# A gated linear recurrence with a ReGLU layer behind it, on one core: one store a chunk, six output buffers, a new instruction order

## The chip, the core and the metric

The kernel runs on one core of a Trainium2 chip. The core has a matrix engine (TensorE, PE in the profile; its weight loads are PEld), a vector engine (VectorE, DVE), a scalar engine (ScalarE, ACT), a general engine (GpSimd, POOL) and a queue engine (SyncE, SP), which here only issues DMA transfers. Each engine works through its own list of instructions in order and waits on semaphores for the others. The metric is the device time of one execution in microseconds (us).

## What is computed

A recurrence over 768 time steps for 4 batches and 8 heads of width 48, and a ReGLU layer of width 1536 over its 3072 output rows of width 384:

```python
f = 1.0 / (1.0 + np.exp(-f_logit))
for t in range(S):
    state = f[:, :, t, :, None] * state + np.einsum('bhd,bhe->bhde', k[:, :, t], v[:, :, t])
    y[:, :, t] = np.einsum('bhd,bhde->bhe', q[:, :, t], state)
x = y.transpose(0, 2, 1, 3).reshape(B * S, H * D)
out = (np.maximum(x @ w_gate, 0.0) * (x @ w_val)) @ w_out
```

Inputs, weights and output are float32 in memory; the matrix products run in bfloat16.

## The kernel before

**Recurrence.** The rows are cut into chunks of 128 time steps, 24 chunks in all; two chunks of one batch make a unit, and the twelve units run in the order of their time, batch by batch (`seq`). `unit(u)` loads f, k, q and v of a unit (4 buffers each), takes exp and logarithm of the gate on ScalarE, sums the logarithms along time with triangular matmuls (L537 to L539, "cumsum"), takes exponentials of the sums (L555, L562), multiplies them onto k and q ("hats", L574 and L580), transposes the result (units 0 to 3 on TensorE, L612, the others by DMA on SP, L623), forms scores (L637), masks them (`ptm`, L646 to L651) and adds the product of scores and v to the product of q and the state (`out_of`, L735 to L746). A decay total per chunk (L674, L678 and the exponential at L683, or a small round trip by DMA) updates the state (L498 to L505).

**Even and odd rows.** A partition of a loaded tile holds two neighbouring time steps. For the chunks in `PE_X` the copy of the result (`xT`) puts the rows back in the order of time; for the other eight the result is transposed by DMA (L765) with the 64 even rows ahead of the 64 odd ones, and the output keeps that order until it is stored.

**ReGLU.** Four chunks make a group; `ffn_hidden(g, r0, r1, j)` makes one of twelve slices of 128 hidden columns: three gate matmuls into a PSUM bank, three value matmuls into another (both L783), relu on ScalarE (L788) and the product on VectorE into `gT` (L790). `ffn_out` makes a chunk's output from twelve slices (L807, four steps of three matmuls), copies the bank to an output buffer `osb` (L393 on ScalarE, L394 on VectorE) and stores the buffer on SP's queue (L828). Chunk `w` uses buffer `w % NO`, with `NO = 4`; the last chunk is done in two pieces of 256 and 128 columns. A chunk in `PE_X` is stored by one transfer of 128 rows, each other chunk by two transfers of 64 rows with a stride of two rows.

**Order.** Nothing is ordered by the code's sequence: each step is entered in a list with what it reads and writes (`Plan.add`), and the constants give the rest. `SEQUENCE` has the order of the steps on each engine, by their numbers; `HOMES` the order in which tiles use the eight PSUM banks; `UNITS` the engine for each copy or product (a name ending in 1 is a copy done as a reduction on VectorE); `FILLERS` the number of matmuls of zeros (L861) that run before a step's other waits; `FIRST` the first loads, with `x@y` for a weight slice x that is issued only once load y has landed. `follow` checks that the lists agree, and `needs` derives the semaphore waits. Weights are loaded by GpSimd's queue (L467), as it converts them to bfloat16; all other transfers are on SP's queue (loads: L453).

At the start VectorE writes the constants (L381, L409, L421), among them `zeros`, which the fillers and one further matmul of zeros into a bank of its own (`hot`, L854) read; that matmul stands in TensorE's list behind the first transposes of unit 0.

Of the kernel before, what the change touches and what calls it, by code (L numbers as in the profile page):

```python
# [37 lines left out]
class Plan:  # L38
# [82 lines left out]
    def needs(self, warm):  # L121
# [69 lines left out]
    "ACT": [  # L191
# [9 lines left out]
    "DVE": [  # L201
# [9 lines left out]
    "POOL": [  # L211
# [38 lines left out]
FILLERS = {67: 4, 105: 1, 82: 4, 89: 4, 86: 1, 124: 1, 127: 1, 151: 1}  # L250
# [23 lines left out]
def bass_hgrn2_outer__then__ffn_reglu_kernel(  # L274
# [11 lines left out]
    C = 128  # L286
# [3 lines left out]
    DM, DFF = w_gate.shape  # L290
# [142 lines left out]
    for i in range(NV):  # L433
        fill(fill_on["vpad"][i], f"vpad{i}", bass.AP(tensor=vpad[i], offset=D, ap=[[VW, 128], [VSTEP, NP], [1, 16]]).bitcast(U32), 0, 32)
# [508 lines left out]
```

## Time and profile before

| | |
|---|---|
| time, median of 3 runs | 193.91 us (192.78 to 194.66) |
| time of the profiled execution | 193.92 us |
| its span, first to last instruction | 192.2 us |
| VectorE, ScalarE, GpSimd busy | 126.2, 116.0, 98.9 us |
| DMA | 32.40 MB, mean 169 GB/s |
| stores of the output | 33 transfers: 15 of 192 KB, 16 of 96 KB, one of 128 KB and one of 64 KB |

The span is cut into 40 equal slices in the page's second part; a digit is the busy share of an engine in that slice, in tenths. TensorE's matmuls are pipelined and their ends are modelled, so its busy time overstates its work. In a timeline each row has the start, the duration, the engine, the line, the operation, the written and read tiles, the shape and the number of merged instructions, and in brackets the idle time of the engine before it and what ended it. "SPq" and "POOLq" are the queues that issue transfers.

### The profile page before, as it was taken

The numbers are of one execution on the slowest core, as the hardware profiler recorded it, in microseconds if no ns is written. First come the engines' busy times: TensorE is split into PE (matmuls) and PEld (weight loads), VectorE is DVE, ScalarE is ACT, GpSimd is POOL, SyncE is SP. The second block draws the span as 40 slices with busy tenths as digits, with TensorE's granted clock in tenths as the row PEclk, the third lists the DMA queues.
The fourth block names the chain that finished last, engine by engine and source line by source line (L and its number), as shares of the span: only waits on it lengthen the run. The fifth ranks groups of instructions, "written<-read, shape, count | busy, mean of one in ns | idle before, by whom it ended". The sixth has DMA issues, their size and how long they took to land.

```text
span 192.2 us, 4338 instructions
## 1 busy us (share of the span) xinstructions
PE 179.4 (93%) x1708; PEld 97.8 (51%) x1708; DVE 126.2 (66%) x233; ACT 116.0 (60%) x227; POOL 98.9 (51%) x132
## 2 busy tenths in 40 slices
PE   0988899999999999989999989999999999999982
PEld 0455674456545464545554535555555554554552
DVE  2589877886797899877784979585177424235501
ACT  4976787894858978975887763682343332224020
POOL 5496756897689679858688994115403200000000
PEclk9999999999999999999999999999999999999999
DMA  6999999999999999999998979532602103000145
GB/s 158 325 290 241 216 230 211 268 172 163 275 285 202 210 327 275 193 213 257 258 293 194 226 151 171 127 82 41 151 3 63 42 0 102 3 0 0 45 119 164
DMA packets 81199, 32.40 MB, mean 169 GB/s; under 512 B 73366, under 2 KB 81180, under 8 KB 81180
## 3 DMA queue, kind: packets, MB, share of 16 engines
q1 hardware_dynamic: 76380, 28.60, 62.3%
q0 software_dynamic: 4800, 3.54, 12.3%
q8 instruction: 13, 0.21, 0.5%
q14 instruction: 6, 0.05, 0.1%
HBM read 25.96 MB, written 4.73 MB: 160 GB/s over the span
## 4 chain that ended last, share of the span: by engine, by line
PE 58%; DMA 21%; SPq 8%; POOL 5%; ACT 2%; issue 2%; DVE 2%; POOLq 0%; ACTq 0%; DVEq 0%
PE ps L783 35%; PE ps L807 16%; DMA out_dram<-osb 7%; DMA k_in<-in_k_dram 6%; DMA wv<-in_moe_w_val_dram 5%; SPq L453 5%; DMA q_in<-in_q_dram 3%; SPq L828 2%; PE ps L637 2%; POOL hats L580 2%; PE ps L735 1%; POOL ptm L648 1%; SPq L623 1%; PE ps L746 1%; ACT relu L788 1%
## 5 line engine op out<-in xcount | busy, mean ns | idle before, releaser
L790 DVE TENSOR_TENSOR gT<-relu,ps 128x512 bf16<-128x512 bf16 (+1 forms) x75 | 47.7, 661 | 21.6 <-PE ps L783 17.4
L788 ACT ACTIVATE relu<-ps 128x512 bf16<-128x512 f32 (+1 forms) x75 | 41.4, 578 | 28.9 <-PE ps L783 17.3
L783 PE MATMUL ps<-xT,wv 128*128 128x512 bf16 (+1 forms) x225 | 55.7, 371 | 0.2 <-DMA wv<-in_moe_w_val_dram 0.2
L783 PE MATMUL ps<-xT,wg 128*128 128x512 bf16 (+1 forms) x225 | 54.8, 371 | 1.1 <-DVE hats L574 0.5
L807 PE MATMUL ps<-wo,gT 128*128 128x384 bf16 (+2 forms) x300 | 52.4, 320 | 0.7 <-ACT osb L393 0.7
L807 PEld LDWEIGHTS ps<-wo,gT 128*128 128x128 bf16 x300 | 28.1, 98 | 20.5 <-ACT osb L393 1.1
L783 PEld LDWEIGHTS ps<-xT,wg 128*128 128x128 bf16 x225 | 21.0, 98 | 23.0 <-DVE hats L574 0.7
L783 PEld LDWEIGHTS ps<-xT,wv 128*128 128x128 bf16 x225 | 20.8, 98 | 21.0 <-issue 0.7
L648 POOL TENSOR_TENSOR ptm<-ptm,seen 128x512 bf16<-128x512 bf16 x21 | 23.9, 1156 | 14.6 <-ACT ptm L646 14.3
L505 POOL TENSOR_TENSOR st<-ssum,dec 128x384 bf16<-128x384 f32 x16 | 13.2, 829 | 18.8 <-DVE ssum L502 11.3
L580 POOL TENSOR_TENSOR hats<-q_in,expo 64x384 bf16<-64x384 f32 x20 | 19.9, 996 | 4.1 <-ACT expo L555 2.2
L651 DVE TENSOR_TENSOR ptm<-ps,seen 128x512 bf16<-128x512 f32 x27 | 17.5, 685 | 2.8 <-PE ps L637 2.5
L394 DVE COPY osb<-ps 128x384 f32<-128x384 f32 (+2 forms) x11 | 5.7, 521 | 20.4 <-PE ps L807 13.5
L580 DVE TENSOR_TENSOR hats<-k_in,ps 64x384 bf16<-64x384 f32 x32 | 17.6, 551 | 1.9 <-ACT ps L562 0.8
L393 ACT ACTIVATE osb<-ps 128x384 f32<-128x384 f32 x14 | 6.7, 490 | 18.7 <-DMA out_dram<-osb 9.9
L646 ACT ACTIVATE ptm<-ps 128x512 bf16<-128x512 f32 x21 | 12.0, 597 | 5.1 <-PE ps L637 5.1
L394 POOL CAST vpad<-v_in 64x384 bf16<-64x384 f32 x20 | 10.5, 524 | 4.3 <-DMA v_in<-in_v_dram 3.3
L555 ACT ACTIVATE expo<-ps 128x384 f32<-128x384 f32 x22 | 10.2, 496 | 1.7 <-DVE ps L544 1.6
L861 PE MATMUL ps<-zeros 128*128 128x512 bf16 x17 | 6.1, 455 | 5.4 <-DVE halves L421 4.6
L574 POOL TENSOR_TENSOR hats<-q_in,expo 128x384 bf16<-128x384 f32 x9 | 9.2, 1032 | 3.3 <-ACT expo L555 2.3
L523 ACT ACTIVATE f_in<-f_in 128x768 f32<-128x768 f32 x12 | 10.0, 839 | 1.5 <-DMA f_in<-in_f_logit_dram 1.4
L562 ACT ACTIVATE ps<-ps 128x384 f32<-128x384 f32 x22 | 10.6, 499 | 0.0
(89 smaller groups left out, 182.0 us busy)
## 6 DMA issues: line engine op xcount, KB each, us to landing
f_in<-in_f_logit_dram SPq DMA_DIRECT2D x12, 384.0 KB, 6.0
v_in<-in_v_dram SPq DMA_DIRECT2D x12, 384.0 KB, 5.0
k_in<-in_k_dram SPq DMA_DIRECT2D x12, 384.0 KB, 4.8
q_in<-in_q_dram SPq DMA_DIRECT2D x12, 384.0 KB, 4.9
out_dram<-osb SPq DMA_DIRECT2D x15, 192.0 KB, 3.1
out_dram<-osb SPq DMA_DIRECT2D x16, 96.0 KB, 2.2
wg<-in_moe_w_gate_dram POOLq DMA_DIRECT2D x4, 288.0 KB, 6.8
wv<-in_moe_w_val_dram POOLq DMA_DIRECT2D x4, 288.0 KB, 7.6
```

The costliest lines, as they stand in the source:

```text
L394: return engine[e].tensor_copy(out, src)
L505: add(e, lambda: engine[e].tensor_tensor(t4(s_new), t4(tmp), rate, ALU.mult), [key] + dk, [f"S{b}_{y}"], **(dict(occ=0.79, lat=0.1) if e = ...
L555: add("ACT", lambda: sc.activation(expo[:, ei, i, 0, :], bc[i].ap[:, 0:HD], AF.Exp, scale=-1.0), [bc[i]], [f"expq{ei}_{i}"], **act_t(HD))
L562: add("ACT", lambda i=i, ex=ex: sc.activation(bc[i].ap[:, 0:HD] if in_place else ex[:, 1, :], bc[i].ap[:, 0:HD], AF.Exp, scale=1.0), [bc[i ...
L580: op = add(e, lambda i=i, n=n, x=x, e=e, y=y, lo=lo, exps=exps: engine[e].tensor_tensor(hats[64 * i:64 * i + 64, hi, y, x, :, 0:D], by_i[n ...
L646: add("ACT", lambda pt=pt, s=sj[j]: sc.activation(pt, s.ap[:, :].rearrange("p (n t) -> p n t", n=NP), AF.Copy), [sj[j]], [f"raw{mis[y]}_{j ...
L648: add("POOL", lambda pt=pt, mask=mask: gp.tensor_tensor(pt, pt, mask, ALU.mult), [f"raw{mis[y]}_{j}", "seen"], [f"raw{mis[y]}_{j}", f"ptm{ ...
L651: add("DVE", lambda pt=pt, mask=mask, s=sj[j]: ve.tensor_tensor(pt, s.ap[:, :].rearrange("p (n t) -> p n t", n=NP), mask, ALU.mult), [sj[j ...
L783: mm = te.matmul(bank.ap[:, 0:n], wt[:, kt, j * 128:(j + 1) * 128], xT[xi][:, kt, n0:n1], start=(kt == 0), stop=(kt == NK - 1))
L788: add("ACT", lambda: sc.activation(relu[ri][:, 0:n], gate.ap[:, 0:n], AF.Relu), [gate], [f"relu{ri}"], **act_t(n))
L790: add("DVE", lambda: ve.tensor_tensor(gT[gi][:, j, n0:n1], relu[ri][:, 0:n], val.ap[:, 0:n], ALU.mult), [val, f"relu{ri}"], [f"gT{gi}_{j}_ ...
L807: mm = te.matmul(bank.ap[:, 0:cut[1] - cut[0]], gT[gi][:, j, r * C:(r + 1) * C], wo[:, j, cut[0]:cut[1]], start=(j == 0), stop=(j == NJ - 1))
```

## The change

- Each chunk's output is stored by one transfer. For a chunk with even rows ahead of odd ones, the target has three dimensions (two row parities, 64 rows, columns).
- `NO` is 6: chunk `w` uses buffer `w % 6`.
- The matmul of zeros into a bank of its own is entered before the units, is the first step in TensorE's list, and the cumsums of unit 0 come after it.
- `SEQUENCE`, `HOMES`, `UNITS`, `FILLERS` and the weight releases in `FIRST` are replaced throughout. There are eight steps fewer on SP. On SP the first loads run f0 v0 f1 v1 q0 k0 k1 f2 q1 in place of f0 f1 v0 k0 q0 k1 q1 f2 v1. The decay totals of units 0 and 1 stand third and seventh in TensorE's list, ahead of the first transposes. On VectorE `zeros` is the eighth step, where it was the seventh.

```diff
-FILLERS = {67: 4, 105: 1, 82: 4, 89: 4, 86: 1, 124: 1, 127: 1, 151: 1}
+FILLERS = {67: 4, 106: 1, 83: 11, 123: 2, 87: 1, 152: 1}
...
-FIRST = 'f0 k0 q0 v0 f1 k1 q1 v1 f2 k2 q2 v2 f3 k3 q3 v3 wg0 wv0 wg1@q0 wv1@k2 wg2 wv2@k1 wg3@k0 wv3@k2 wo0@q3 wo1@v1 wo2@f1 wo3@f3'
+FIRST = 'f0 k0 q0 v0 f1 k1 q1 v1 f2 k2 q2 v2 f3 k3 q3 v3 wg0@k0 wv0@k0 wg1@q1 wv1 wg2@k1 wv2@k2 wg3@q1 wv3 wo0@f2 wo1@k0 wo2@q2 wo3@k1'
...
-    NO = 4
+    NO = 6
...
+    WARM = 512
+    hot = Bank("hot")
+    first_pe = add("PE", lambda: te.matmul(hot.ap[:, 0:WARM], zeros[:, 0:128], zeros[:, 0:WARM]), ["zeros"], [hot], occ=0.2, opens=[hot])
...
-            add("PE", cum, bkeys + ["upto", "below"], [bc[i]], occ=0.17 if on["sum"] else 0.33, lat=PE_L,
+            add("PE", cum, bkeys + ["upto", "below"], [bc[i]], after=[first_pe] if u == 0 else [], occ=0.17 if on["sum"] else 0.33, lat=PE_L,
...
-                for i in range(1 if w in pe_x else 2):
-                    whole = w in pe_x
-                    dst = bass.AP(tensor=out.tensor, offset=base + i * DM, ap=[[DM if whole else 2 * DM, C if whole else C // 2], [1, wide]])
-                    src = osb[oi][:, cut[0]:cut[1]] if whole else osb[oi][64 * i:64 * i + 64, cut[0]:cut[1]]
-                    op = add("SP", lambda dst=dst, src=src: sy.dma_start(dst, src), [f"osb{oi}_{n}"], [f"out{w}_{i}_{n}"],
-                             occ=0.36, lat=0.9)
-                    dma(op, f"osb{oi}_{i}_{n}", (0.6 if whole else 0.42) * wide / DM, 1)
+                if w in pe_x:
+                    dst = bass.AP(tensor=out.tensor, offset=base, ap=[[DM, C], [1, wide]])
+                    src = osb[oi][:, cut[0]:cut[1]]
+                else:
+                    dst = bass.AP(tensor=out.tensor, offset=base, ap=[[DM, 2], [2 * DM, C // 2], [1, wide]])
+                    src = osb[oi][:, cut[0]:cut[1]]
+                op = add("SP", lambda dst=dst, src=src: sy.dma_start(dst, src), [f"osb{oi}_{n}"], [f"out{w}_{n}"], occ=0.36, lat=0.9)
+                dma(op, f"osb{oi}_{n}", 0.6 * wide / DM, 1)
...
-    WARM = 512
-    hot = Bank("hot")
-    add("PE", lambda: te.matmul(hot.ap[:, 0:WARM], zeros[:, 0:128], zeros[:, 0:WARM]), ["zeros"], [hot], occ=0.2, opens=[hot])
```

The replaced lists are too long to show. What the prediction uses of them it names by steps. At the end of SP's list the stores now run by chunk: 16, 17, 18, 19, 20, 22, 21 and the two pieces of 23; before, they ran 17 (second half), 18 (second), 17, 16 (second), 16, 19, 18, 19 (second), 22, 20, 21 (second), 21, 20 (second) and the two pieces of 23.

More of the change, by code (lines that the diff above doesn't have):

```diff
@@ L234 @@
-    [
-        0, 9, 11, 19, 62, 31, 37, 44, 50, 78, 82, 58, 129, 90, 119, 130, 106, 163, 144, 169, 138, 179, 172, 212, 159, 160, 188, 215, 222, 217,
-        209, 266, 232, 237, 269, 242, 273, 275, 282, 285, 287, 301, 297],
-    [
-        1, 8, 6, 5, 28, 22, 25, 34, 66, 43, 47, 51, 71, 113, 92, 93, 99, 116, 105, 143, 166, 175, 152, 150, 257, 214, 200, 207, 208, 210, 231,
-        230, 244, 265, 248, 298, 293],
-    [
-        13, 16, 18, 70, 27, 33, 67, 83, 48, 84, 56, 57, 102, 115, 110, 122, 173, 146, 178, 153, 156, 185, 226, 193, 223, 198, 262, 202, 203, 239,
-        270, 247, 274, 276, 284],
@@ L243 @@
-    [
-        308, 15, 17, 24, 38, 76, 77, 81, 85, 59, 123, 91, 97, 128, 108, 121, 174, 164, 149, 171, 147, 158, 192, 189, 196, 197, 228, 267, 236,
-        253, 240, 280, 251, 283, 278, 286, 300],
-    [
-        3, 12, 61, 30, 26, 32, 68, 41, 54, 72, 74, 112, 89, 96, 131, 104, 162, 135, 140, 167, 148, 176, 221, 154, 258, 213, 191, 218, 201, 194,
-        259, 199, 245, 238, 246, 290, 292, 294, 296, 303],
+        1, 8, 71, 13, 25, 28, 70, 38, 44, 78, 72, 52, 86, 124, 96, 132, 126, 163, 112, 142, 170, 139, 172, 159, 184, 185, 192, 227, 218, 229,
@@ new lines @@
+        228, 263, 246, 238, 245, 252, 270, 278, 289],
+    [
+        10, 61, 29, 66, 34, 43, 40, 55, 80, 56, 60, 95, 90, 94, 105, 117, 104, 123, 135, 166, 150, 147, 152, 161, 155, 259, 194, 197, 199, 268,
+        230, 232, 241, 299, 277, 303],
+    [
+        22, 3, 16, 21, 63, 30, 39, 45, 41, 48, 83, 58, 89, 91, 99, 131, 106, 169, 134, 137, 167, 181, 153, 222, 186, 190, 196, 223, 200, 203,
+        211, 239, 271, 256, 283, 301, 287, 307],
+    [
+        14, 6, 19, 62, 32, 36, 42, 53, 75, 119, 125, 100, 102, 118, 129, 164, 140, 165, 180, 176, 154, 182, 160, 183, 191, 193, 224, 205, 264,
+        208, 262, 209, 204, 240, 242, 266, 273, 285, 284, 292],
@@ new lines @@
+    [
+        11, 5, 27, 35, 37, 76, 49, 50, 73, 85, 57, 98, 116, 128, 122, 174, 141, 149, 178, 212, 157, 189, 188, 217, 202, 195, 260, 236, 243, 254,
+        248, 257, 279, 286, 280, 295, 298, 305],
+    [
+        15, 4, 20, 23, 26, 33, 65, 68, 47, 79, 81, 87, 113, 93, 120, 101, 107, 111, 175, 145, 138, 146, 173, 158, 151, 214, 201, 225, 210, 267,
+        233, 251, 272, 265, 250, 274, 294, 302, 288, 297],
+    [
+        0, 9, 12, 31, 67, 77, 46, 54, 88, 114, 97, 121, 115, 127, 133, 108, 110, 136, 143, 168, 177, 213, 162, 187, 216, 226, 207, 234, 247, 269,
+        255, 275, 290, 291, 293, 300, 296, 306],
@@ L249 @@
+    [
+        2, 7, 17, 18, 24, 64, 69, 84, 51, 82, 74, 59, 92, 130, 103, 109, 144, 171, 179, 148, 156, 221, 258, 215, 198, 219, 206, 220, 261, 235,
+        231, 237, 244, 253, 249, 281, 282, 276, 304, 308],
 ]
[L250 removed]
+FILLERS = {67: 4, 106: 1, 83: 11, 123: 2, 87: 1, 152: 1}
 UNITS = {
[3 rows of a table removed]
[L256 to L264 removed]
@@ new lines @@
+    0: {'kps': False, 'qps': False, 'q0': 'DVE', 'q1': 'POOL', 'even': 'PE', 'm00': 'DVE', 'm01': 'DVE', 'm10': 'DVE', 'tk': 'ACT', 'm11': 'DVE', 'r1': 'POOL', 'tq': 'DVE', 'v11': 'DVE1', 'v10': 'POOL', 'r0': 'DVE1', 'v01': 'DVE1', 'v00': 'DVE1', 'vb': 'DVE1', 'pr': False, 'o1': 'ACT', 'vc0': 'DVE', 'x0': 'ACT', 'x1': 'ACT', 'yy': True, 'o0': 'DVE', 'vc1': 'ACT', 'td': False, 'k0': 'DVE', 'k1': 'POOL'},
+    1: {'kps': True, 'r0': 'DVE1', 'm01': 'DVE', 'm00': 'DVE', 'tq': 'ACT', 'v11': 'DVE1', 'even': 'PE', 'tk': 'DVE', 'q1': 'POOL', 'v00': 'DVE1', 'm11': 'POOL', 'r1': 'ACT', 'm10': 'DVE', 'v01': 'POOL', 'v10': 'ACT', 'q0': 'POOL', 'qps': False, 'yy': False, 'td': False, 'vb': 'DVE', 'vc0': 'DVE', 'o0': 'ACT', 'vc1': 'DVE', 'x0': 'DVE', 'o1': 'ACT', 'x1': 'ACT'},
@@ new lines @@
+    2: {'tk': 'DVE', 'v01': 'ACT', 'kps': True, 'r1': 'ACT', 'r0': 'POOL', 'even': 'PE', 'q0': 'DVE', 'v00': 'POOL', 'v10': 'POOL', 'm00': 'DVE', 'v11': 'POOL', 'm01': 'POOL', 'm11': 'POOL', 'tq': 'DVE', 'q1': 'POOL', 'm10': 'POOL', 'qps': True, 'x0': 'ACT', 'vc1': 'ACT', 'pr': False, 'vc0': 'DVE', 'o0': 'ACT', 'x1': 'DVE', 'vb': 'POOL', 'o1': 'ACT'},
+    3: {'kps': True, 'm00': 'DVE', 'm11': 'POOL', 'v11': 'ACT', 'm10': 'POOL', 'tk': 'DVE', 'v01': 'DVE1', 'r1': 'ACT', 'tq': 'ACT', 'q1': 'POOL', 'v00': 'ACT', 'v10': 'POOL', 'q0': 'DVE', 'r0': 'POOL', 'm01': 'DVE', 'even': 'DVE', 'qps': False, 'vb': 'DVE1', 'x1': 'DVE', 'o1': 'DVE', 'vc1': 'ACT', 'pr': False, 'vc0': 'DVE', 'o0': 'ACT', 'x0': 'ACT', 'sum': 'POOL'},
@@ new lines @@
+    4: {'v10': 'POOL', 'v01': 'POOL', 'm00': 'DVE', 'q11': 'POOL', 'q00': 'POOL', 'q01': 'POOL', 'q0': 'POOL', 'kps': True, 'even': 'DVE', 'm01': 'DVE', 'v00': 'POOL', 'm10': 'POOL', 'q10': 'POOL', 'q1': 'POOL', 'm11': 'POOL', 'v11': 'ACT', 'qps': False, 'tq': 'DVE', 'r0': 'ACT', 'tk': 'DVE', 'r1': 'ACT', 'yy': True, 'o1': 'ACT', 'o0': 'ACT', 'x1': 'ACT', 'x0': 'DVE', 'sum': 'POOL'},
+    5: {'q1': 'POOL', 'm00': 'DVE', 'kps': True, 'q11': 'POOL', 'v10': 'ACT', 'v00': 'ACT', 'even': 'DVE', 'q01': 'POOL', 'm11': 'POOL', 'q00': 'POOL', 'q0': 'POOL', 'v11': 'POOL', 'm01': 'DVE', 'q10': 'POOL', 'v01': 'ACT', 'm10': 'DVE', 'tq': 'ACT', 'r0': 'ACT', 'tk': 'DVE', 'r1': 'POOL', 'qps': False, 'o1': 'DVE', 'x0': 'DVE', 'o0': 'ACT', 'yy': False, 'x1': 'ACT', 'sum': 'DVE'},
@@ new lines @@
+    6: {'v10': 'POOL', 'v01': 'POOL', 'q10': 'POOL', 'm10': 'DVE', 'kps': True, 'q1': 'POOL', 'even': 'DVE', 'q01': 'POOL', 'm00': 'POOL', 'm01': 'POOL', 'q11': 'POOL', 'q00': 'POOL', 'm11': 'POOL', 'qps': False, 'q0': 'POOL', 'pr': False, 'o0': 'DVE', 'yy': False, 'o1': 'DVE', 'v11': 'POOL', 'x0': 'DVE', 'v00': 'ACT', 'x1': 'DVE', 'sum': 'POOL'},
+    7: {'v10': 'DVE1', 'kps': True, 'q1': 'POOL', 'v01': 'DVE1', 'q11': 'POOL', 'm00': 'DVE', 'v11': 'ACT', 'even': 'DVE', 'm10': 'POOL', 'm11': 'DVE', 'm01': 'POOL', 'q10': 'POOL', 'qps': False, 'q01': 'POOL', 'q0': 'POOL', 'o0': 'ACT', 'x1': 'ACT', 'td': True, 'x0': 'ACT', 'o1': 'ACT', 'v00': 'DVE1', 'sum': 'POOL'},
@@ new lines @@
+    8: {'m10': 'DVE', 'v11': 'ACT', 'q01': 'POOL', 'm01': 'POOL', 'even': 'DVE', 'q0': 'POOL', 'v10': 'ACT', 'q1': 'POOL', 'm00': 'DVE', 'kps': True, 'q11': 'POOL', 'q00': 'POOL', 'qps': False, 'v00': 'POOL', 'q10': 'POOL', 'v01': 'POOL', 'pr': False, 'td': True, 'x0': 'DVE', 'o1': 'ACT', 'x1': 'ACT', 'o0': 'ACT', 'sum': 'POOL'},
+    9: {'v11': 'POOL', 'v10': 'ACT', 'even': 'DVE', 'kps': True, 'q1': 'POOL', 'm10': 'DVE', 'v00': 'ACT', 'm11': 'POOL', 'q11': 'POOL', 'm00': 'DVE', 'q00': 'POOL', 'q10': 'POOL', 'q0': 'POOL', 'q01': 'POOL', 'v01': 'ACT', 'm01': 'DVE', 'yy': False, 'x0': 'ACT', 'td': True, 'o0': 'DVE', 'x1': 'DVE', 'o1': 'DVE', 'sum': 'POOL'},
@@ new lines @@
+    10: {'m00': 'POOL', 'm10': 'POOL', 'q0': 'POOL', 'kps': True, 'q10': 'POOL', 'm01': 'POOL', 'q11': 'POOL', 'q00': 'POOL', 'v11': 'ACT', 'even': 'DVE', 'v01': 'ACT', 'v00': 'DVE1', 'q01': 'POOL', 'q1': 'POOL', 'm11': 'DVE', 'v10': 'DVE1', 'td': True, 'o0': 'DVE', 'x0': 'DVE', 'x1': 'DVE', 'o1': 'ACT', 'sum': 'POOL'},
+    11: {'q0': 'POOL', 'v01': 'DVE1', 'q10': 'POOL', 'm00': 'DVE', 'q01': 'POOL', 'm11': 'POOL', 'q1': 'POOL', 'q00': 'POOL', 'kps': True, 'v11': 'DVE1', 'm01': 'DVE', 'q11': 'POOL', 'even': 'DVE', 'v00': 'ACT', 'm10': 'POOL', 'v10': 'ACT', 'yy': True, 'o1': 'ACT', 'td': True, 'x0': 'DVE', 'x1': 'DVE', 'o0': 'ACT', 'sum': 'POOL'},
```

15 lines of the change are left out of this document (removed), and 85 rows, old and new, of tables (SEQUENCE, UNITS).

## The prediction

> **What bounds the kernel now.** I read the page first, then the waits of TensorE, then the timeline of its end, its middle and its start.
>
> ```profile
> span 192.2 us, 4338 instructions
> ...
> PE 179.4 (93%) x1708; PEld 97.8 (51%) x1708; DVE 126.2 (66%) x233; ACT 116.0 (60%) x227; POOL 98.9 (51%) x132
> ...
> PE   0988899999999999989999989999999999999982
> ...
> PEclk9999999999999999999999999999999999999999
> ```
>
> TensorE is the engine that is full: only the first slice (4.8 us each) and the last are empty, and no other engine passes two thirds. The matrix products stay the same in the change, so what can be won or lost is time in which TensorE does not work: the start, the pauses, and the end behind its last matmul. The waits of TensorE name the pauses (waiting line, releaser: us in total, times, longest):
>
> ```profile
> PE ps L861 <- DVE halves L421: 4.6, 1, 4.6
> PE ps L807 <- ACT osb L393: 0.7, 1, 0.7
> ...
> PE ps L783 <- DVE osb L394: 0.5, 1, 0.5
> ```
>
> Two of them end with a copy into an output buffer (osb), and so are about the part that gets six buffers. The end, as a timeline (start, duration, engine, line; in brackets the idle time before and what ended it), and the row of the store line in that stretch (min/median/max ns, first and last start):
>
> ```profile
> 180.01 10.44 SPq L828 DMA_DIRECT2D out_dram<-osb  x15
> ...
> 180.84 5.04 PE L807 MATMUL ps<-wo,gT 128*128 128x384 bf16 x30
> ...
> 186.04 0.87 ACT L393 ACTIVATE osb<-ps 128x384 f32<-128x384 f32 x2 [0.81 <-DMA out_dram<-osb]
> ...
> 186.58 2.15 PE L807 MATMUL ps<-wo,gT 128*128 128x256 bf16 x24 [0.70 <-ACT osb L393]
> 188.11 0.43 DVE L394 COPY osb<-ps 128x256 f32<-128x256 f32 x1 [6.37 <-PE ps L807]
> 188.78 0.29 DVE L394 COPY osb<-ps 128x128 f32<-128x128 f32 x1 [0.24 <-PE ps L807]
> ```
> ```profile
> L828 SPq DMA_DIRECT2D out_dram<-osb x15: 338/597/604, 180.0 to 190.0; - x15
> ```
>
> Fifteen stores queue on SP from 180.01, each holding the queue 0.597 us. ScalarE's copy at 186.04 needs a buffer whose store is in that queue; TensorE needs the PSUM bank that this copy empties and pauses 0.70 us. The last copy is over at 188.78 + 0.29 = 189.07, but the last store starts at 190.0, since others are ahead of it.
>
> **The change part by part.** The sum is made against the profiled execution's own time, 193.92 us: its span of 192.2 and 1.72 around it; the median of the runs shown, 193.91, is the same.
>
> *End: one store a chunk, six buffers, new order.* The last eight chunks (16 to 23) made fifteen stores; now they make nine. Chunk 20 to 23 take buffers 2 to 5, last used by chunks 14 to 17, whose stores stand well ahead. So the copy at 186.04 has nothing to wait for: -0.70. At the very end the queue holds chunks 20, 22 and 21 and the two pieces of 23, one store each; at 0.6 us each they are through when the last copy ends: 190.0 - 189.07 = 0.93, less an issue gap: -0.9. Both pieces of 23 now go to ScalarE in place of VectorE; whole-chunk copies take 0.87 us for two there, so I put that at 0. Together -1.6; it could be 0 only if another queue took SP's place, and I see none.
>
> *One store in place of two, elsewhere.*
>
> ```profile
> out_dram<-osb SPq DMA_DIRECT2D x15, 192.0 KB, 3.1
> out_dram<-osb SPq DMA_DIRECT2D x16, 96.0 KB, 2.2
> ```
>
> Eight chunks lose one issue each, 8 x 0.597 = 4.8 us of SP's time. SP is seldom the last to be waited for, so that is not on the path. A buffer is free 3.1 us after one issue, where it was free 0.6 + 2.2 = 2.8 after the first of two: 0.3 later, under the cover of two more buffers; without them it would be paid at each osb wait.
>
> *Middle.*
>
> ```profile
> 80.71 1.30 SPq L623 DMA_TRANSPOSE qkT<-hats  x1
> ...
> 82.15 0.62 PE L637 MATMUL ps<-qkT 48*128 48x128 bf16 x16 [0.45 <-issue]
> 82.66 0.56 DVE L394 COPY osb<-ps 128x384 f32<-128x384 f32 x1 [1.10 <-DMA out_dram<-osb]
> ...
> 83.28 0.82 PE L783 MATMUL ps<-xT,wg 128*128 128x512 bf16 x3 [0.50 <-DVE osb L394]
> ```
> ```profile
> 108.96 0.49 ACT L393 ACTIVATE osb<-ps 128x384 f32<-128x384 f32 x1 [1.25 <-DMA out_dram<-osb]
> ...
> 111.18 0.40 PE L637 MATMUL ps<-qkT 48*128 48x128 bf16 x8 [0.38 <-DVE ssum L502]
> ...
> 111.88 0.40 PE L637 MATMUL ps<-qkT 48*128 48x128 bf16 x8 [0.30 <-ACT relu L788]
> ```
>
> VectorE's copy at 82.66 waited 1.10 for a store, and TensorE 0.50 behind it for the bank. With six buffers the chunk needs a store two chunks older: -0.50. At 82.15 TensorE waits 0.45 for scores whose transpose went out late on SP, and at 111 it waits 0.38 + 0.30 for engines held up by ScalarE's 1.25 for a store. These 1.13 us hang on the store queue only in part: between 0 and -1.13 I take half, -0.57.
>
> *Start.* What moves: the zeros' matmul opens TensorE's list, v0 and v1 go ahead of q0 and k0 on SP's queue (k0 from the fourth load to the sixth), weights are released by other loads, and both decay totals of units 0 and 1 go ahead of the first transposes.
>
> ```profile
> 3.09 1.15 SPq L453 DMA_DIRECT2D k_in<-in_k_dram  x1
> ...
> 4.57 1.89 PE L861 MATMUL ps<-zeros 128*128 128x512 bf16 x4 [4.57 <-DVE halves L421]
> ...
> 5.21 0.84 ACT L530 ACTIVATE bneg<-f_in 128x768 bf16<-128x768 f32 x1
> ...
> 5.48 1.15 SPq L453 DMA_DIRECT2D k_in<-in_k_dram  x1
> ...
> 8.35 1.00 POOL L574 TENSOR_TENSOR hats<-k_in,expo 128x384 bf16<-128x384 f32 x1 [0.70 <-ACT expo L562]
> ...
> 9.15 1.03 PE L861 MATMUL ps<-zeros 128*128 128x512 bf16 x4
> 9.31 1.31 POOL L574 TENSOR_TENSOR hats<-q_in,expo 128x384 bf16<-128x384 f32 x1
> ...
> 10.57 0.93 POOL L467 DMA_DIRECT2D wg<-in_moe_w_gate_dram  x1
> ...
> 11.19 0.61 PE L612 MATMUL ps<-ident,hats 128*128 128x128 bf16 x8 [0.34 <-DVE hats L574]
> ...
> 11.49 0.78 POOL L467 DMA_DIRECT2D wv<-in_moe_w_val_dram  x1
> ...
> 12.32 0.50 POOL L394 CAST vrest<-v_in 64x384 bf16<-64x384 f32 x1
> 12.91 1.96 POOL L574 TENSOR_TENSOR hats<-q_in,expo 128x384 bf16<-128x384 f32 x2
> ```
> ```profile
> 16.64 0.17 PE L674 MATMUL ps<-away,other 128*128 128x16 bf16 x1
> 16.67 0.34 PE L678 MATMUL ps<-halves,bneg 128*128 128x4 bf16 x8
> ```
>
> Zeros earlier are worth 0: the first product with data needs the logarithm, which ends at 5.21 + 0.84 = 6.05 and is not touched. The first four zero products took 1.89 us at 4.57 and 1.03 at 9.15: TensorE runs at half pace for its first 4.5 us. [...]
>
> The decay total of unit 0 stood beside a wait already; that of unit 1 at 16.64 lay in TensorE's busy stretch: -0.3 (0 to -0.7).
>
> Against this stands k0. Its load is issued in the place of 5.48 in place of 3.09, 2.39 us later. Landing times of k in the first 40 us, and of the value weights:
>
> ```profile
> DMA to landing us min/median/max: 4.8/7.1/10.9
> ```
> ```profile
> DMA to landing us min/median/max: 6.9/7.6/10.1
> ```
>
> With the shortest landing, k0 was there at 7.9, ahead of the product at 8.35, and will be at 10.3. On POOL the k product (1.00) and the q product (1.31) follow: 12.6, where TensorE began the q transposes at 11.19: +1.4. Eleven filler products, not four, stand ahead of the k transposes for it; behind them the lists hold four fillers where eight stood, and four cost 1.03 us by the row at 9.15. Part of those filled a wait, so I count 0.75 of it as won. So +0.65, between 0 (TensorE would wait for the first weights anyway) and +2.4 (the whole delay). Queued behind k0's wait are, on POOL, vrest and the weights, on VectorE the k products of unit 1; the release of wg0 by k0 adds nothing, since the k product stands ahead of it on POOL.
>
> *Everything else that was reordered* does the same work with the same matmuls. Its cost is only new or lost pauses; I take 0, with -1 to +2 about it.
>
> Sum: -1.6 - 0.50 - 0.57 - 0.3 + 0.65 = -2.3, so 193.92 - 2.3 = **191.6 us**.
>
> **The rivals.**
>
> *The store queue gets a new wait (no change).* Chunk 5's store now stands only three places ahead of chunk 11's on SP, and both use buffer 5. So chunk 11's copy, on VectorE, waits out 3.1 us of chunk 5's landing, and behind chunk 11's store stand the transposes of unit 11. For it: every osb wait above is of this kind. Against: unit 11 has other chunks' output between it and its need. Paid by half, +1.6: 193.2 (192.6 to 194.7).
>
> *The first value weights come late (slower).* With k0 at 10.3, POOL issues wg0 at 10.3 + 1.00 + 1.31 + 0.50 = 13.1 and, behind 0.93 of that issue and the two q products of unit 1 (1.96), wv0 at 16.0 in place of 11.49. It lands at 23.6 by the median, 26.1 by the longest.
>
> ```profile
> 20.45 0.49 PE L783 MATMUL ps<-xT,wv 128*128 128x256 bf16 x3
> ```
>
> That is its first use now. The new list puts two more gate triples and two chunk outputs ahead of it, some 0.5 us each by this row: needed at about 20.45 + 1.4 + 2 = 23.8. At the medians it is just in time. It decides where k0 lands later than about 10.5: with k0 at its median landing (5.48 + 7.1 = 12.6) all is 2.3 later, and with wv0's longest landing another 2.5: +4.6 or so, 193.92 - 2.3 + 4.6 = 196.2 (194.0 to 198). For it: the landings scatter this much. Against: wg1, wg2 and wv1 go out sooner than before, so the stretch after it has more to work on.
>
> [...]
>
> *More goes than I count (faster still).* All of 1.13 in the middle, 0.7 of the totals, no loss at the start, and a pause or two more: 193.92 - 1.6 - 0.5 - 1.1 - 0.7 = 190.0 (188.9 to 190.6).
>
> **How the numbers follow.** Forecast (190.6 to 192.6) 0.47, new store wait 0.17, late value weights 0.18, clock 0.04, more than counted 0.14. Measurements of this kernel scatter by about 1% (192.78 to 194.66), so no change means 191.97 to 195.85. Faster: 0.34 of the forecast's 0.47 and all of the 0.14: 0.48. Slower: two thirds of the late weights and 0.02 of the store wait: 0.14. The rest, 0.38, is no change. For 8 in 10 I leave out the lower 0.06 of the best case and 0.12 of the slow one: 189.3 to 195.6.
>
> **What would show it.** TensorE without a wait on an osb copy, and no osb copy waiting for a store, show the buffers; the last store starting within 0.1 us of the last copy's end shows the end. TensorE's first q transposes at 12 to 13, and the first value product without a wait at 23 to 24, show the start; a wait on wv there longer than 1 us, or on k or q products, shows the slow rival. SP sitting at chunk 11's store, with VectorE's copy waiting for out_dram, shows the other. A new pause of TensorE over 1 us past 40 us, in a stretch I put at 0, would make the forecast wrong by a step that it did not name.

## The result and the profile after

The changed kernel takes **204.99 us** (median of 4 runs, 204.12 to 205.48) against 193.9 us of the kernel before in the same comparison: a ratio of 1.057 with a 95% interval of [1.051, 1.064]. It is slower by 11 us; the prediction had said 191.6 us, in a range that ended at 195.6. The profiled execution took 205.48 us, 11.6 more than that of before. Here and below a ratio compares the fast runs of two kernels alone while a median is over all runs, so a ratio can differ from the quotient of two medians (for the kernel with two halves the medians of 193.01 and 193.31 us would give 0.998, where the ratio is 0.991).

The page of the changed kernel, first lines, TensorE's slices, its granted clock, and the row of the stores:

```profile
span 203.8 us, 4318 instructions
...
PE 179.5 (88%) x1689; PEld 98.9 (49%) x1711; DVE 127.7 (63%) x235; ACT 118.4 (58%) x230; POOL 96.7 (47%) x127
...
PE   2887899999999999999999993999999999999600
...
PEclk9999999999999999999999997699999999999975
...
out_dram<-osb SPq DMA_DIRECT2D x23, 192.0 KB
```

TensorE's busy time is that of before (179.4). The time came in two places that the slices show (a digit is now 5.1 us): a hole at the 25th slice, near 125 us, with a granted clock of 0.7 and 0.6 there and behind it, and two empty slices at the end. Most of what follows is about these two.

The end, as a timeline, and what the DMA engines moved from 183 us to the end of the span in 40 slices of 0.52 us (GB/s):

```profile
183.81 12.11 SPq L834 DMA_DIRECT2D out_dram<-osb  x7
...
190.73 0.49 ACT L393 ACTIVATE osb<-ps 128x384 f32<-128x384 f32 x1 [3.25 <-PE ps L811]
191.38 0.38 ACT L393 ACTIVATE osb<-ps 128x256 f32<-128x256 f32 x1 [0.16 <-PE ps L811]
192.05 0.28 ACT L393 ACTIVATE osb<-ps 128x128 f32<-128x128 f32 x1 [0.29 <-PE ps L811]
```
```profile
GB/s 0 0 0 12 18 41 24 32 32 50 50 50 50 50 50 50 56 86 284 95 62 50 50 50 56 257 144 62 57 56 38 50 50 50 50 50 50 45 8 0
```

These copies into the buffers wait for TensorE's banks alone (the brackets), as forecast, and the last one ends at 192.05 + 0.28 = 192.33. But the span ends 11.5 us later, where before it ended 3.1 us after the last copy (189.07 to 192.2). In between the DMA engines do one thing: they move 50 GB/s, slice after slice. The two peaks fit the stores of plain rows in between, chunk 22 and the pieces of chunk 23. The four chunks in even-odd order that stand in this queue (18 to 21) have 4 x 196,608 bytes; at 50 GB/s that takes 15.7 us, from 184 us on. The last store starts at about 195.5, some 3 us behind the last copy, where the prediction had asked for 0.1.

The middle, as a timeline, and two windows (start and end, length, then busy time and count for PE, PEld, DVE, ACT and POOL, granted clock, DMA share, GB/s):

```profile
123.68 0.33 PE L746 MATMUL ps<-st,qkT 128*128 128x96 bf16 x4 [1.69 <-POOL st L509]
...
125.40 0.56 DVE L394 CAST xn<-ps 128x384 bf16<-128x384 f32 x1 [4.52 <-DMA xT<-xn]
...
126.01 0.50 PE L746 MATMUL ps<-st,qkT 128*128 128x96 bf16 x4 [1.80 <-DVE xn L394]
```
```profile
120.00:125.00 5.00, 2.52 (x36) 1.56 (x34) 0.69 (x1) 0.98 (x2) 0.83 (x1) 0.95 0.72 75
125.00:130.00 5.00, 3.77 (x21) 2.13 (x23) 2.73 (x5) 2.34 (x6) 0.00 (x0) 0.50 0.79 209
```

TensorE waits 1.69 us for a state and 1.80 us for a result that waits 4.52 us for a transpose; then it runs at half clock for some five microseconds. The prediction had counted no cost in this stretch.

### The profile page after: what moved, and what is told of

It is laid out like the page before. It is cut to its first block, busy times and chain, and to the rows that moved or that the text cites. A ratio compares the mean times of both kernels' runs of the same rounds, so it can differ in the third digit from the quotient of the medians.

```text
span 203.8 us, 4318 instructions
## 1 busy us (share of the span) xinstructions
PE 179.5 (88%) x1689; PEld 98.9 (49%) x1711; DVE 127.7 (63%) x235; ACT 118.4 (58%) x230; POOL 96.7 (47%) x127
## 3 DMA queue, kind: packets, MB, share of 16 engines
q0 software_dynamic: 4800, 3.54, 11.6%
## 5 line engine op out<-in xcount | busy, mean ns | idle before, releaser
L794 DVE TENSOR_TENSOR gT<-relu,ps 128x512 bf16<-128x512 bf16 (+1 forms) x75 | 48.5, 663 | 29.1 <-PE ps L787 18.4
L792 ACT ACTIVATE relu<-ps 128x512 bf16<-128x512 f32 (+1 forms) x75 | 42.2, 580 | 36.3 <-PE ps L787 25.5
L811 PE MATMUL ps<-wo,gT 128*128 128x384 bf16 (+2 forms) x300 | 54.9, 327 | 0.0
L787 PE MATMUL ps<-xT,wv 128*128 128x512 bf16 (+1 forms) x217 | 53.4, 371 | 1.0 <-DMA wv<-in_moe_w_val_dram 0.4
L811 PEld LDWEIGHTS ps<-wo,gT 128*128 128x128 bf16 x300 | 28.8, 100 | 21.5 <-issue 2.2
L652 POOL TENSOR_TENSOR ptm<-ptm,seen 128x512 bf16<-128x512 bf16 x21 | 24.0, 1154 | 14.8 <-ACT ptm L650 14.7
L393 ACT ACTIVATE osb<-ps 128x384 f32<-128x384 f32 (+2 forms) x17 | 7.9, 471 | 15.6 <-PE ps L811 13.8
L393 ACT ACTIVATE vpad<-v_in 64x384 bf16<-64x384 f32 x19 | 9.8, 517 | 1.8 <-DMA v_in<-in_v_dram 1.0
L578 POOL TENSOR_TENSOR hats<-q_in,expo 128x384 bf16<-128x384 f32 x10 | 10.2, 1027 | 0.8 <-DMA q_in<-in_q_dram 0.5
L531 POOL TENSOR_TENSOR bneg<-f_in 128x384 bf16<-128x384 f32 x8 | 8.0, 998 | 3.9 <-ACT f_in L529 3.9
L506 DVE TENSOR_TENSOR ssum<-ps,st 128x384 f32<-128x384 f32 x16 | 8.8, 549 | 1.0 <-POOL st L509 0.7
```

The lines of the kernel that those rows point to most:

```text
L393: return sc.activation(out, src, AF.Copy)
L652: add("POOL", lambda pt=pt, mask=mask: gp.tensor_tensor(pt, pt, mask, ALU.mult), [f"raw{mis[y]}_{j}", "seen"], [f"raw{mis[y]}_{j}", f"ptm{ ...
L787: mm = te.matmul(bank.ap[:, 0:n], wt[:, kt, j * 128:(j + 1) * 128], xT[xi][:, kt, n0:n1], start=(kt == 0), stop=(kt == NK - 1))
L792: add("ACT", lambda: sc.activation(relu[ri][:, 0:n], gate.ap[:, 0:n], AF.Relu), [gate], [f"relu{ri}"], **act_t(n))
L794: add("DVE", lambda: ve.tensor_tensor(gT[gi][:, j, n0:n1], relu[ri][:, 0:n], val.ap[:, 0:n], ALU.mult), [val, f"relu{ri}"], [f"gT{gi}_{j}_ ...
L811: mm = te.matmul(bank.ap[:, 0:cut[1] - cut[0]], gT[gi][:, j, r * C:(r + 1) * C], wo[:, j, cut[0]:cut[1]], start=(j == 0), stop=(j == NJ - 1))
```

## Experiments

The theories. **A:** the store with the target cut 2 x 64 x columns is slow in itself, some 50 GB/s; that makes the end, and in the middle chunk 6's store holds up what is issued behind it. **B:** the new order, the six buffers or the new start made both. **C:** a variant of A, in which rows that stand two rows apart are slow to write however they are cut.

### Undoing the one store alone

```diff
-dst = bass.AP(tensor=out.tensor, offset=base, ap=[[DM, 2], [2 * DM, C // 2], [1, wide]])
-src = osb[oi][:, cut[0]:cut[1]]
+dst = bass.AP(tensor=out.tensor, offset=base, ap=[[2 * DM, C // 2], [1, wide]])
+src = osb[oi][0:64, cut[0]:cut[1]]
...
+ins.then_inc(slots[f"osb{oi}_{n}"][0], 16)
+ins = sy.dma_start(odd_rows, osb[oi][64:128, cut[0]:cut[1]])
```

> The changed kernel with its one store a chunk undone: each of the eight chunks in even-odd row order (6, 14, 16 to 21) goes out by two stores of 64 partitions again, both issued in the place of the one, all else as in the changed kernel. Theory A (a store whose target is cut 2 x 64 x columns moves at some 50 GB/s, 192 KB in 3.9 us; five or six of them pile up at the end, and one in the middle holds up the small transfers behind it): the end's 8.6 us and the middle's 4 us go, 190 to 193.5 us, last landing 2 to 4 us after the last copy, and no stall at 121 us. Theory B (the searched order, six buffers or the start cost the time): 200 us or more, with the stall at 121 us still there. Theory C (rows of the target that stand two rows apart are slow to write however they are cut): 200 us or more, the end still late.

Measured: 193.01 us (median of 10 runs, 190.1 to 198.84), a ratio of 0.991 [0.986, 0.996] to the kernel before. The end and the middle of this kernel:

```profile
185.82 0.28 ACT L393 ACTIVATE osb<-ps 128x128 f32<-128x128 f32 x1 [0.29 <-PE ps L811]
186.16 1.08 SPq L838 DMA_DIRECT2D out_dram<-osb  x2
```
```profile
span 189.0 us, 4326 instructions
```
```profile
120.00:125.00 5.00, 4.94 (x62) 3.27 (x61) 3.42 (x6) 2.83 (x7) 0.75 (x1) 1.00 0.88 148
125.00:130.00 5.00, 4.95 (x39) 2.53 (x39) 3.61 (x7) 3.26 (x7) 3.51 (x4) 1.00 0.47 142
```

The last copy ends at 186.10, 6.2 us sooner than in the changed kernel, and the span 2.9 us behind it, 8.6 us less: together the 14.8 us between the two spans. No pause between 120 and 130 us, full clock. B and C fall: order, buffers and start are those of the changed kernel, and the rows are written two apart as in it.

### The same stores to plain rows

```diff
-dst = bass.AP(tensor=out.tensor, offset=base, ap=[[DM, 2], [2 * DM, C // 2], [1, wide]])
+dst = bass.AP(tensor=out.tensor, offset=base, ap=[[DM, C], [1, wide]])
```

> The changed kernel with the target of those eight stores written as 128 rows in a row, still one store a chunk (rows of these eight chunks stay in even-odd order in the output; as many bytes, as many instructions). Theory A: the slowest dimension is 128 in place of 2, a store is as fast as the other sixteen chunks' stores, 190 to 193 us, at most 1 us off the kernel with two halves. Theory B: 200 us or more. Theory C: 190 to 193 us too, so that this kernel and the one with two halves together tell A from C.

Measured: 191.06 us (189.29 to 192.42), a ratio of 0.987 [0.980, 0.994]. One store a chunk costs nothing overall; that shape of target does. (Here, and with the cuts below, the rows of these chunks land in another order than the wanted one; as many bytes are moved.)

### The slowest dimension: 8 and 4 in place of 2

```diff
-ap=[[DM, 2], [2 * DM, C // 2], [1, wide]]
+ap=[[DM, 8], [8 * DM, C // 8], [1, wide]]
```

> The changed kernel with the target of those eight stores cut 8 x 16 x columns in place of 2 x 64 x columns, rows of one cut eight apart (the rows of these eight chunks land in another order; as many bytes, as many instructions). The same three-dimensional form with a wider stride: only the slowest dimension differs. Theory A: the rate goes with that dimension, four times some 50 GB/s, 192 KB in about 1 us: no pile at the end, 190.5 to 194 us. Theory C, or if three dimensions are what is slow: 203 us or more, no better than the changed kernel. Theory B: 200 us or more.

> The changed kernel with the target of the eight stores cut 4 x 32 x columns (rows of these chunks land in another order). Theory A: twice the changed kernel's 50 GB/s in the tail, 100 GB/s, 2 us for a store; the four last take 8 us from about 181 us on, which is about when the last copies come anyway, so the end costs 0 to 1.5 us over the cut in eight, and the middle stall lies between that kernel's 1.75 us and the changed kernel's: 192 to 196 us. If the rate did not go with the slowest dimension but fell only at 2: 191 to 193.5 us with some 200 GB/s in the tail.

Measured: cut in eight 192.63 us, 0.996 [0.993, 0.999]; cut in four 195.63 us, 1.015 [1.009, 1.020]. What the DMA engines move while these stores drain tells it best. First chunks 16 and 17, between 170 and 180 us (slices of 0.25 us), in the changed kernel and with the cut in four:

```profile
GB/s 0 0 0 0 0 0 25 12 78 49 31 18 37 12 49 43 18 49 49 49 49 55 49 49 49 49 49 49 55 49 49 49 49 49 55 49 49 49 49 49
```
```profile
GB/s 18 31 49 68 86 92 98 98 98 98 104 98 98 98 98 111 98 49 6 0 0 0 0 0 0 0 0 0 0 0 0 0 0 0 0 0 0 0 0 0
```

The row "DMA" of the same two views, in tenths of the 16 engines that are busy:

```profile
DMA  0000000131010111011111111111111111111111
```
```profile
DMA  3122222222222222210000000000000000000000
```

Then the last stores with the cut in eight and with plain rows (178 to 191 us, up to the span's end; slices of some 0.3 us):

```profile
GB/s 0 0 0 0 0 0 0 52 57 43 165 203 189 198 194 109 0 0 0 0 0 0 0 43 57 47 213 383 255 194 76 52 54 252 336 268 164 28 0 0
```
```profile
GB/s 0 0 0 0 0 312 364 378 156 0 0 0 0 0 0 0 0 0 0 0 0 260 369 378 203 0 0 5 336 322 331 148 70 0 0 0 0 0 0 0
```

The plateaus are 49, 98, some 195 and some 370 GB/s for a slowest dimension of 2, 4, 8 and 128: 24.5 GB/s for each unit up to 8, then no more than some fifteen times it. The row "DMA" stands at 1 of 10 beside the 49 (0.13 over 175 to 180 us, or 2.1 of sixteen engines) and at 2 of 10 beside the 98 (0.2 to 0.3, or 3.2 to 4.8 engines), which fits two and four engines; in the other two views it is 5 beside the 195 and up to 9 beside the 370. That the number of busy engines goes with the slowest dimension is read from these four shapes; what sets it, no run shows.

The middle has the same order, with two halves above all of these. TensorE's busy time between 120 and 130 us was 6.29 us with a slowest dimension of 2 (2.52 + 3.77 above), 7.34 with 4, 8.11 with 8, 8.90 with plain rows and 9.89 with two halves, by one profile each.

### The one store alone, in the old kernel

```diff
+if i:
+    add("SP", None).skip = True
+    continue
...
+dst = bass.AP(tensor=out.tensor, offset=base, ap=[[DM, C], [1, wide]] if whole else [[DM, 2], [2 * DM, C // 2], [1, wide]])
+src = osb[oi][:, cut[0]:cut[1]]
```

> The kernel before with one thing of the change alone: one store a chunk with the target cut 2 x 64 x columns, in the place where the first of the two stores stood; old order, four output buffers, old start. Theory A: six stores of 3.9 us one after another from about 165 us on, and with four buffers the copies wait for them as well: 200 to 212 us, with a pause of TensorE or ScalarE on the output buffers that the changed kernel didn't have. Theory B: 193 to 195 us, since the order, the buffers and the start are the old ones.

Measured: 217.68 us (216.61 to 219.95), a ratio of 1.126 [1.119, 1.133]. The wait at the copies came as expected, but its price was above the range of 200 to 212 us. The waits in its profile, taken of the run of 219.95 us (waiting line, releaser: us in total, times, longest):

```profile
ACT osb L394 <- DMA out_dram<-osb: 31.4, 5, 12.7
...
PE ps L808 <- ACT osb L394: 14.2, 2, 13.1
```

TensorE stands 13.1 us behind one copy. In the changed kernel, with six buffers and its own order, TensorE has no such wait, and the kernel is 12.7 us faster than this one.

### Middle and end apart

The store by two halves again for all chunks but 6, and for chunk 6 alone:

```diff
...
+two = w not in pe_x and w > 6
...
```
```diff
...
+two = w not in pe_x and w == 6
...
```

> The changed kernel with two stores again for chunks 14 and 16 to 21, and the one store cut 2 x 64 x columns kept for chunk 6 alone (issued near 114 us, behind it the decay's small transfer at 115 us and the transposes at 118 and 121 us). Theory A: the end is mended (last copy to the end of the span 3 us, not 11.7), the stall between 120 and 130 us and the clock's fall after it stay, some 6 us by the two profiles' last copies (192.05 against 185.82 us): 195.5 to 198.5 us. If that stall has another cause than chunk 6's store, it is gone or there whatever chunk 6 does: 190 to 193.5 us, or the same stall in the kernel that mends chunk 6 alone.

> The other half: two stores again for chunk 6 alone, the one store cut 2 x 64 x columns kept for chunks 14 and 16 to 21. Theory A: no stall between 120 and 130 us, the clock stays open; the last four such stores (18, 19, 20, 21) still go one behind the other at 50 GB/s, 15.7 us for their 786 KB from about 180 us on: 196.5 to 201 us, with 8 to 12 us between the last copy and the end. The rival, that the stall is not chunk 6's: 203 us or more, the stall still there.

Measured: 196.4 us, 1.017 [1.011, 1.023], with the end mended, and 199.43 us, 1.033 [1.027, 1.039], with chunk 6 mended. Last copy and end of the span, first for the end mended, then for chunk 6 mended:

```profile
191.61 0.28 ACT L393 ACTIVATE osb<-ps 128x128 f32<-128x128 f32 x1 [0.28 <-PE ps L811]
```
```profile
span 194.7 us, 4325 instructions
```
```profile
185.35 0.28 ACT L393 ACTIVATE osb<-ps 128x128 f32<-128x128 f32 x1 [0.28 <-PE ps L811]
```
```profile
span 197.0 us, 4319 instructions
```

2.8 us against 11.4 us behind the last copy; a last copy at 191.89 against 185.63. So chunk 6's one store moves everything behind it by 6 us, and the later ones cost the end 8.6. In ratios to the kernel before: 1.0572 less 1.0170 is 0.040 for the end, 1.0572 less 1.0325 is 0.025 for the middle, together 0.065; undoing both gave 1.0572 less 0.9911, or 0.066.

How one store reaches TensorE six microseconds on is read from SP's queue behind it. In the changed kernel (the second of the two stores at 113.68 is chunk 6's):

```profile
113.68 1.08 SPq L834 DMA_DIRECT2D out_dram<-osb  x2
114.80 0.50 SPq L457 DMA_DIRECT2D q_in<-in_q_dram  x1
115.35 2.61 SPq L671 DMA_DIRECT2D dec<-rates  x1
118.01 3.42 SPq L627 DMA_TRANSPOSE qkT<-hats  x1
121.47 1.26 SPq L769 DMA_TRANSPOSE xT<-xn  x1
```

And with two halves for every chunk:

```profile
116.27 0.73 SPq L671 DMA_DIRECT2D dec<-rates  x1
117.04 1.30 SPq L627 DMA_TRANSPOSE qkT<-hats  x1
118.39 1.26 SPq L769 DMA_TRANSPOSE xT<-xn  x1
```

The issue of the small decay transfer takes 2.61 us in place of 0.73, that of the transpose 3.42 in place of 1.30, and the transpose behind TensorE's second pause goes out 3.08 us later. The decay transfers themselves also land late. Between 110 and 124 us, in the changed kernel and with two halves:

```profile
DMA to landing us min/median/max: 2.8/3.2/7.2
```
```profile
DMA to landing us min/median/max: 3.1/3.4/3.5
```

The longest fits the last of them: issued at 115.35, there at about 122.5, and GpSimd's update of the state, for which TensorE's first pause waits, starts at 122.71. The longest is 7.2 us as well where chunk 6's store is kept and the end mended, and 3.5 us where chunk 6 is mended.

Not all of the delay belongs to the shape, though. With plain rows, still one store:

```profile
116.19 2.43 SPq L627 DMA_TRANSPOSE qkT<-hats  x1
118.66 1.26 SPq L769 DMA_TRANSPOSE xT<-xn  x1
```

The decay's issue takes 0.67 us there, but the transpose's still 2.43, and the next one lands 4.1 us after its issue, where with two halves the longest is 2.7. TensorE waits 0.9 us for that result, and not at all with two halves. Why one fast store lengthens these is not shown.

So the slow store's cost was not only its own landing: what its queue issued next went out late (3.42 us for the transpose's issue in place of 1.30) and landed late (7.2 us for the decay in place of 3.5 at most). That this comes from the two engines or so (0.13 of sixteen, above) that still had the store's rows to move is argued from this, not shown.

### What the rest of the change is worth

> The kernel before with six output buffers in place of four, alone: old order, old start, two stores a chunk. By the forecast's terms the pauses of TensorE on the output buffers go (0.70 us at 186.58, 0.50 us at 82.66), and the copies at the end no longer wait: 0.5 to 1.5 us less, 191.7 to 193 us. The rival, that these pauses are made up later or the order holds the same time anyway: within 0.3 us of the kernel before.

```diff
-    NO = 4
+    NO = 6
```

Measured: 191.31 us, 0.993 [0.989, 0.996], a little under the range (by the ratio, 192.5 of 193.9 us, inside it); TensorE no longer waits for an output buffer.

> The kernel before with one store a chunk as 128 rows in a row, in the place of the first of the two (rows of the eight chunks stay in even-odd order): old order, four buffers, old start. This is the one store as the forecast took it, fast. If its price was right, buffers come free 1 to 2 us sooner and the end's queue of stores shrinks: 191.3 to 192.8 us. The rival, that with four buffers the release was not what the end waits for: within 0.3 us of the kernel before. Against the 217.7 us of the same kernel with the cut 2 x 64 x columns, either way 24 us or more lie between two ways to write one target.

```diff
+if i:
+    add("SP", None).skip = True
+    continue
...
-dst = bass.AP(tensor=out.tensor, offset=base + i * DM, ap=[[DM if whole else 2 * DM, C if whole else C // 2], [1, wide]])
...
+dst = bass.AP(tensor=out.tensor, offset=base, ap=[[DM, C], [1, wide]] if whole else [[DM, C], [1, wide]])
+src = osb[oi][:, cut[0]:cut[1]]
```

Measured: 190.56 us, 0.989 [0.986, 0.993], again a little under the range (by the ratio, 191.8 of 193.9 us, inside it). A fast single store is worth about 1%, in the old order and with four buffers.

### Versions that keep one store and have the rows in time order

The rows can be put in order before the store. Both versions also leave xT in even-odd order for all chunks and store every chunk as 128 plain rows; the lines shown are what differs. First in the moving operand of the two first products of the ReGLU layer:

```diff
-mm = te.matmul(bank.ap[:, 0:n], wt[:, kt, j * 128:(j + 1) * 128], xT[xi][:, kt, n0:n1],
+mm = te.matmul(bank.ap[:, 0:n], wt[:, kt, j * 128:(j + 1) * 128], xT[xi][:, kt, n0:n1].rearrange("p (r i t) -> p r t i", i=2, t=C // 2),
```

> A version that might beat both: the changed kernel with every chunk of xT left in even-odd order (the transposed copy of the sixteen other chunks writes straight, too), the first two products of the gated layer reading their moving operand in time order (pairs of columns 64 apart), and every chunk stored in one piece as 128 rows in a row. If TensorE reads such a pattern at the same pace (0.21 us apart for 512 columns): 189.5 to 192.5 us, at or a little below the kernel with plain stores. The rival: the pattern slows the 450 matmuls; 5% on their 96 us is 5 us, 196 us, and half pace 280 us or more.

Measured: 304.14 us, 1.575 [1.567, 1.583]: the hoped-for range was missed, and the rival's half pace came. The gate matmuls of 512 columns (busy time, mean ns of one) in the changed kernel and here:

```profile
L787 PE MATMUL ps<-xT,wg 128*128 128x512 bf16 x195 | 51.5, 382 | 0.9 <-DVE ps L548 0.2 <-issue 0.2
```
```profile
L787 PE MATMUL ps<-xT,wg 128*128 128x512 bf16 x207 | 108.1, 645 | 0.0
```

Then in VectorE's product that writes `gT`:

```diff
-add("DVE", lambda: ve.tensor_tensor(gT[gi][:, j, n0:n1], relu[ri][:, 0:n], val.ap[:, 0:n], ALU.mult),
+def eo(ap):
+    return ap.rearrange("p (r i t) -> p r i t", i=2, t=C // 2)
+lined = gT[gi][:, j, n0:n1].rearrange("p (r t i) -> p r i t", i=2, t=C // 2)
+add("DVE", lambda: ve.tensor_tensor(lined, eo(relu[ri][:, 0:n]), eo(val.ap[:, 0:n]), ALU.mult),
```

> A version that might beat both, the rows put back in another place: xT is left in even-odd order for all chunks as in the kernel with the reordered moving operand, but the two products read it straight; VectorE's product of the gated layer writes gT in time order (every second bf16 of a run, 4 bytes apart), and every chunk is stored in one piece as 128 rows in a row. The 75 products of VectorE take 663 ns each now and it idles some 29 us before them, so even 20% more (10 us in all) lies mostly in idle time: 189.5 to 192.5 us, a ratio of 0.980 to 0.993. The rival: VectorE writes two-byte values apart at half pace, the products take 1.2 us and TensorE waits for gT: 197 us or more.

Measured: 190.16 us (189.17 to 191.76), 0.987 [0.982, 0.992]. The products take 705 ns in the mean in place of 663 (75 times 42 ns, 3.2 us of VectorE), under the cover of its idle time:

```profile
L797 DVE TENSOR_TENSOR gT<-relu,ps 128x512 bf16<-128x512 bf16 (+1 forms) x75 | 51.1, 705 | 28.4 <-PE ps L787 18.2 <-ACT relu L792 9.6
```

It is faster than both kernels of the case, than the one before by 1.3%. At last the same parts in the old order, with the old start:

> The old order and the old start with what helped alone: six output buffers, VectorE's product of the gated layer writing gT in time order, one store a chunk as 128 rows in a row in the place of the first of the two. If the gains of six buffers (0.9927) and of the fast single store (0.9894) add, 0.982, 189.5 us; if they are the same gain twice (both free the buffers sooner), 0.987 to 0.991, 190.5 to 191.2 us. Against the kernel with the same parts in the new order and start (0.987): equal within 0.5% means that the searched order and the zeros written first are worth nothing that can be measured; 0.995 or more means that they carry the gain.

Measured: 191.63 us, 0.989 [0.985, 0.993]. The sum of the two gains, 0.982, lies outside the interval, so they overlap, unless the reordered product costs something in this order; in the new order it cost nothing that can be seen (0.987 with plain rows alone and with it). The new order and start are worth nothing that these intervals can tell: 0.987 [0.982, 0.992] with them.

## Why the prediction was wrong

**The step that failed** is in "One store in place of two, elsewhere": "a buffer is free 3.1 us after one issue". The 3.1 us came from the row of fifteen stores of 192 KB, all of them to 128 plain rows. The new store has the same bytes and another shape. The only transfers of before with a slowest dimension of 2 are five of 3 KB (`rates`), too small to show a rate: the price had to be bounded, and no bound was put. Measured, it drains at 49 GB/s, 4 us a chunk.

**The end** stood on that step: "at 0.6 us each they are through", and a worse outcome only "if another queue took SP's place, and I see none". The 0.6 us is what an issue takes on SP; what the end waits for in its place is the DMA engines, which move 50 GB/s. The term was -1.6 us, of which -0.9 stood for the stretch behind the last copy; that stretch turned into +8.4 (11.5 us in place of 3.1).

**Middle and "everything else that was reordered"**, taken at 0 with +2 at most: one slow store there cost 6 us. No rival named it; the one that came nearest, a new wait on the store queue behind chunk 5, put it in another place and at 1.6 us. It did not come: no copy of VectorE waits for a store. The prediction's own sign for a step that it did not name, a new pause of TensorE over 1 us past 40 us, came twice (1.69 and 1.80 us).

**What held.** With the same stores to plain rows, which is the store that the sum had in mind, the ratio is 0.987 [0.980, 0.994], against 191.6 / 193.92 = 0.988. By that run's profile the last copy ends at 187.35 (1.7 us sooner than before; the terms ahead of it make -1.4) and the span 2.1 us behind it (1.1 less; -0.9 was forecast), with the last store starting at 187.38, at once behind the last copy. Six buffers alone gave 0.7% or 1.4 us, by the forecast 0.70 + 0.50, and TensorE waits for no output copy in the changed kernel. That the sum comes out is in part luck: the start was mis-sized (below), and the middle term counted on ScalarE's wait for a store near 109 us going. It stayed, 1.25 us before and 1.74 after, though TensorE no longer waits behind it:

```profile
109.11 0.49 ACT L393 ACTIVATE osb<-ps 128x384 f32<-128x384 f32 x1 [1.74 <-DMA out_dram<-osb]
```

**The start** went in the direction given, and was mis-sized. The wait for k0 came as described: with two halves GpSimd's k product starts at 10.44, behind k0's landing (10.3 in the prediction), and the first transposes at 12.59. The first gate matmul, in the kernel before and with two halves:

```profile
L783 PEld LDWEIGHTS ps<-xT,wg x225: 95/98/99, 19.9 to 176.7; 128*128 128x128 bf16 x113
```
```profile
L787 PEld LDWEIGHTS ps<-xT,wg x225: 95/98/99, 21.5 to 177.4; 128*128 128x128 bf16 x113
```

1.6 us later (2.0 in the changed kernel, at 21.9), where +0.65 stood, inside its bounds of 0 and +2.4. Some of that is only order: the same list starts its last gate matmul 0.7 us later and its last copy 3.0 us sooner than before. The rival of the late value weights fell: TensorE waits 0.4 us for them in the changed kernel, where more than 1 us would have spoken for it.

**The clock.** The chances give it 0.04, a term that no run shows: in the kernel before the granted clock is 9 tenths or more in all forty slices, and at the start of the changed kernel the eleven zero products at 10.25, behind a pause of 0.64 us, took 2.55 us, about the pace of four in 1.03 before. What the changed kernel showed in its place is a fall much later: between 125 and 130 us, behind two pauses of 1.69 and 1.80 us with some 0.5 us of work between them, the granted clock is 0.50, and with chunk 6 mended it is 1.00. How long it lasted (windows of the changed kernel, as above):

```profile
126.00:131.00 5.00, 4.77 (x24) 2.58 (x26) 2.12 (x4) 2.63 (x6) 0.00 (x0) 0.50 0.63 179
131.00:132.00 1.00, 1.00 (x17) 0.54 (x17) 0.00 (x0) 0.00 (x0) 0.00 (x0) 0.86 0.38 89
```

The 0.86 puts the return to full clock near 131.3, so TensorE was busy for some 5 us at half clock, which would have taken 2.5 us at full: an estimate. With the two pauses that makes 6.0 of the 6.2 us by which the last copies differ. The clock made the slow store dearer; it was not the cause.

## What to carry to other kernels

Price a transfer by its shape, not by its bytes: stores of 192 KB went at 49 GB/s to a target with a slowest dimension of 2 and at some 370 to 128 rows. Look at the slowest dimension of the target, the side that was varied here, and if the trace has no transfer with that dimension, bound the price from the 24.5 GB/s for each unit that the cuts in 2, 4 and 8 showed. Where two orders meet in a store, two stores of 64 partitions beat one that starts with a dimension of 2 (0.991 against 1.057); to put the order right in an engine that has idle time, where a strided write cost 6%, did at least as well (0.987 against 0.991, with intervals that overlap). The slow store also delayed what its queue issued next, so the first to suffer was a small urgent transfer behind it (0.8 KB, there after 7.2 us, where 3.5 was the longest with two halves).

## What the runs showed of the hardware that was not expected

- A DMA to a target whose slowest dimension is 2, 4 or 8 moved 49, 98 and some 195 GB/s, one to 128 rows some 370.
- Behind a store with a slowest dimension of 2 SP's issues lengthened: 2.61 us in place of 0.73 and 3.42 in place of 1.30 (2.43 behind a store of plain rows), a small transfer landed after 7.2 us, where 3.5 was the longest with two halves, and in the tail one issue took 3.65.
- TensorE's moving operand with neighbouring columns 128 bytes apart took 645 ns a matmul of 512 columns in place of 382, and the kernel 304 us. VectorE's write of every second bf16 cost 42 ns on a mean of 663.
- Two pauses of TensorE of 1.69 and 1.80 us, with some 0.5 us of work between them, were followed by a granted clock of 0.50 up to about 131.3 us.
